# A spectral and FFN kernel on one core: another order of the first loads, a buffer per scaled matrix, and one block of dummy products

## Chip, cores, metric

The kernel runs on one core of one Trainium2 chip. The metric is device time in microseconds (us), less is better. Engines are named as in the profile: PE (TensorE products), PEld (its weight loads), DVE (VectorE), ACT (ScalarE), POOL (GpSimd), SP (SyncE, which here only issues DMAs).

## What is computed

x is 2048 x 448 in bf16 (batch 1). Two kinds of layer alternate, each with a residual sum around it:

```python
def _A_ref(x, w_r, w_i):
    X = rfft2(x.astype(float32)); X = X * (w_r + 1j * w_i)
    return irfft2(X, s=(S, D)).astype(bfloat16)
def _B_ref(x, w1, b1, w2, b2):
    h = einsum("bsd,df->bsf", x, w1) + b1
    r = where(h > 0, h, 0)
    return einsum("bsf,fd->bsd", r * r, w2) + b2
x = x + _A_ref(layernorm(x), A_w_r, A_w_i)
x = x + _B_ref(layernorm(x), B_w1, B_b1, B_w2, B_b2)
# and both once more with the same weights
```

w_r and w_i are 2048 x 225, w1 is 448 x 1792, w2 1792 x 448. The layernorm has no parameters (eps 1e-5).

## The kernel before

x lies in SBUF as 16 tiles of 128 rows x 448 (partition p holds the rows 16p to 16p+15, tile t is the t-th of each). The Fourier transforms are products with constant matrices, in stages:

- **A1** (`ln_stats` L774, `minus` L803, `first_A` L816): for each tile or pair of tiles (GROUPS1) the mean and the variance, on DVE (bn_stats, bn_aggr) or, for tiles 1, 4 and 6, on ACT (two passes with an accumulator, L781); a square root on ACT, a reciprocal on DVE; then FA (a 16-point transform, 128 x 256) is scaled by the reciprocal (`scaled`, L668, written to a buffer Fs of which there are four, t % NFS). A product on PE is five matmuls of 256 columns: four with the tile, one that subtracts the mean. The result is evacuated to XA by ACT or DVE.
- **TD** multiplies XA along the columns (TD_sb), first the half with tiles 0 to 7, then the one with 8 to 15; it needs the tiles of its half. **B** is the second transform along the rows (G_sb). **W** is the multiplication by w_r and w_i on DVE (`stage_W`, L946). It reads Wt: slots loaded by DMA (Wp), and slots that POOL copies (tags M) out of two gathers (`gather`, L700, tag pool.yT) which fetch the mirrored rows of w_i and w_r.
- **Bi**, **TI**, **AI** go back, with H_sb, HS_sb, TI_sb and FI_sb. **ln**, **h** and **o** are the FFN. Then A2 to AI and the FFN once more.

The order of the work is written out by hand. Every piece of work is a unit with a tag, such as `A1.0`; the table ORDER gives for each tag the ranks of its units, in the order in which the code makes them. A letter behind a rank chooses the engine (a ACT, d DVE, p POOL). Each engine runs its units in the order of rank, in order; a unit waits by semaphores for what it reads and for buffers. For a single tile on DVE the units of `A1.t` are: statistics, aggregate, square root (ACT), reciprocal, minus (-2 x mean), scaled matrix, product (PE), evacuation. For a pair such as `A1.14`: statistics and aggregate of the first tile, of the second, root, reciprocal, minus, then scaled matrix, product and evacuation of the first and of the second.

`schedule` (L415) walks the ranked units with estimated durations. It chooses the PSUM bank (8 of them) for each product, and where PE would by its estimate stand idle it puts in dummies (`warm_mm`, L1306): matmuls of a matrix of ones into a free bank, whose result nobody reads.

The loads (`dma`, L616) go out on SP's and ACT's queues. Before:

```python
for n, (a, b, e) in enumerate(((0, 1, "sp"), (1, 2, "act"), (2, 3, "sp"), (4, 8, "act"), (3, 4, "sp"), (8, 12, "act"),
                               (12, 16, "sp"))):
    dma(e, xin[:, a:b, :], x_dram[:, a:b, :])
    if n == 2: dma("sp", FA_sb[:], dc["FA"])
```

so SP issues x0, x2, FA, x3 and x12 to 15, ACT x1, x4 to 7, a first use of its square root (which loads its table), and x8 to 11. All weight loads (G, TD, Wt, H, HS, ...) are on SP behind these and wait for x4 (`x4`, L747); so do the gathers on POOL.

Of the kernel before, what the change touches and what calls it, by code (L numbers as in the profile page):

```python
# [10 lines left out]
P = 128  # L11
# [30 lines left out]
def make_constants():  # L42
# [71 lines left out]
    for g, M in enumerate((cl * np.cos(th), cl * np.sin(th))):  # L114
# [1270 lines left out]
```

## Time and profile before

| | |
|---|---|
| runs | 266.96 us median of 3 (266.46, 266.96, 268.15) |
| profiled execution | span 267.8 us from the first to the last instruction; its own time is not listed beside it |
| busy | PE 259.3 (97%), PEld 158.9 (59%), DVE 212.7 (79%), ACT 171.3 (64%), POOL 14.4 (5%) |
| dummies | 16, of 512 columns, the last begins at 11.5 us |
| DMA | 17.03 MB, mean 64 GB/s |
| the most waited for | ACT arena on PE 17.7 us, DVE arena on ACT 17.6 us, both spread over the whole span |

Busy time of PE includes the dummies and is modelled where matmuls overlap, so 97% doesn't say that PE is the bound everywhere. In the lines of a timeline the columns are: start, busy time, engine, line, operation, output<-input, shape, count, and in brackets the idle time before with what ended it. The lines of DMA issues have the size of each and the time from issue to landing. A "q" behind an engine is its sequencer, which issues DMAs.

### The profile page before, as it was taken

The page shows a single profiled execution, that of the slowest core. Times are in us where ns is not written, and L with a number is a line of the kernel's source. Part 1 is how long each engine was busy: PE and PEld are TensorE (multiplying, and loading weights), DVE is VectorE, ACT ScalarE, POOL GpSimd, SP SyncE. Part 2 cuts the span into 40 slices and gives each one's busy share as a digit, 9 for nine tenths or more (in the row PEclk, how much of TensorE's full clock was granted, in tenths as well). Part 3 has the DMA queues.
Part 4 walks back from the last instruction along what each step waited for, and adds up shares of the span by engine and source line. Part 5 has one row for each costly group of instructions (what it writes and reads, how often), then busy time and mean ns, then how long its engine had stood idle before and what let it go on. Part 6 is the DMA issues. An engine that isn't in the chain of part 4 may idle for free. (4 is left out here: it accounts for less than half of the span.)

```text
span 267.8 us, 5840 instructions
## 1 busy us (share of the span) xinstructions
PE 259.3 (97%) x2194; PEld 158.9 (59%) x2194; DVE 212.7 (79%) x652; ACT 171.3 (64%) x391; POOL 14.4 (5%) x42
## 2 busy tenths in 40 slices
PE   6899999899999999999999999989999999999996
PEld 1477665798544544555559774779654554454554
DVE  5866999899996964999999899899998963463722
ACT  4688994979429755985128896889735753678000
POOL 0577000000000000000000000000000000000000
PEclk9999999999999999999999999999999999999999
DMA  6999370020420222300000000011232026200211
GB/s 222 305 376 354 74 228 17 0 42 10 54 52 2 39 43 44 68 0 0 2 0 4 2 2 0 2 23 22 39 73 42 0 42 111 89 2 0 70 39 47
DMA packets 27312, 17.03 MB, mean 64 GB/s; under 512 B 20210, under 2 KB 25810, under 8 KB 27156
## 3 DMA queue, kind: packets, MB, share of 16 engines
q1 hardware_dynamic: 26692, 14.82, 21.7%
q10 hardware_dynamic: 432, 1.03, 1.1%
q0 software_dynamic: 160, 0.81, 0.8%
q8 instruction: 17, 0.28, 0.5%
q14 instruction: 11, 0.09, 0.1%
HBM read 11.15 MB, written 1.84 MB: 48 GB/s over the span
## 5 line engine op out<-in xcount | busy, mean ns | idle before, releaser
L636 PE MATMUL ps<-yT,W_sb 64*128 64x512 bf16 (+1 forms) x770 | 90.3, 346 | 0.0
L636 PE MATMUL ps<-W_sb,arena 128*128 128x448 bf16 (+2 forms) x490 | 87.5, 336 | 0.0
L636 PEld LDWEIGHTS ps<-yT,W_sb 64*128 64x128 bf16 (+1 forms) x770 | 51.5, 95 | 36.0 <-issue 1.5
L636 PEld LDWEIGHTS ps<-W_sb,arena 128*128 128x128 bf16 x490 | 46.3, 98 | 36.3 <-DVE arena L688 0.8
L655 ACT ACTIVATE arena<-ps,b1col 128x512 bf16<-128x512 f32 x84 | 51.9, 691 | 14.2 <-PE ps L636 14.0
L688 DVE TENSOR_TENSOR arena<-arena 128x512 bf16<-128x512 bf16 (+1 forms) x140 | 45.7, 367 | 18.0 <-ACT arena L655 17.6
L1109 ACT ACTIVATE VT<-x_sb 128x448 bf16<-128x448 bf16 x32 | 18.4, 577 | 13.4 <-DVE x_sb L1085 13.3
L661 ACT ACTIVATE arena<-ps 128x448 bf16<-128x448 f32 (+1 forms) x44 | 25.1, 693 | 2.4 <-PE ps L636 2.2
L1205 DVE SCALAR_TENSOR_TENSOR x_sb<-ps,arena 128x448 bf16<-128x448 f32 (+2 forms) x27 | 15.2, 570 | 14.1 <-PE ps L636 13.7
L655 ACT ACTIVATE mv<-mv,epst 128x1 f32<-128x1 f32 (+1 forms) x46 | 12.6, 294 | 17.2 <-DVE mv L794 12.1
L655 ACT ACTIVATE arena<-ps 128x256 bf16<-128x256 f32 x56 | 17.8, 392 | 4.0 <-PE ps L636 3.7
L661 ACT ACTIVATE XA<-ps 128x512 bf16<-128x512 f32 x29 | 15.6, 592 | 3.2 <-PE ps L636 3.2
L661 ACT ACTIVATE VT<-ps 128x512 bf16<-128x512 f32 (+1 forms) x26 | 13.0, 567 | 7.0 <-PE ps L636 6.9
L636 PE MATMUL ps<-yT,VT 64*128 64x512 bf16 x42 | 15.8, 376 | 0.0
L636 PE MATMUL ps<-HS_sb,arena 128*128 128x512 bf16 x64 | 14.9, 380 | 0.1
L636 PE MATMUL ps<-arena,G_sb 128*128 128x448 bf16 (+1 forms) x76 | 14.4, 333 | 0.5 <-ACT arena L661 0.4
L672 ACT ACTIVATE arena<-x_sb,rstd 128x448 bf16<-128x448 bf16 x11 | 7.2, 666 | 10.5 <-DVE rstd L1124 6.0
L636 PE MATMUL ps<-TD_sb,XA 112*64 112x112 bf16 (+2 forms) x312 | 13.2, 224 | 0.0
L636 PE MATMUL ps<-Fs,xin 128*128 128x256 bf16 x64 | 10.0, 290 | 3.0 <-DVE mv L784 2.9
L636 PEld LDWEIGHTS ps<-TD_sb,XA 112*64 112x64 bf16 (+2 forms) x312 | 12.1, 108 | 1.1 <-issue 0.6
L688 DVE TENSOR_TENSOR tmp<-arena,Wt 128x896 bf16<-128x896 bf16 (+1 forms) x14 | 11.4, 852 | 1.7 <-ACT arena L661 1.5
L1135 DVE SCALAR_TENSOR_TENSOR arena<-x_sb,mv,b2row 128x448 bf16<-128x448 bf16 x16 | 10.7, 679 | 0.1
(76 smaller groups left out, 300.9 us busy)
## 6 DMA issues: line engine op xcount, KB each, us to landing
out_dram<-x_sb SPq DMA_DIRECT2D x15, 112.0 KB, 1.7
W_sb<-in_B_w_dram SPq DMA_DIRECT2D x1, 1568.0 KB, 16.1
W_sb<-in_B_w_dram SPq DMA_DIRECT2D x1, 1344.0 KB, 6.7
HS_sb<-c_HS SPq DMA_DIRECT2D x1, 1024.0 KB, 11.2
G_sb<-c_G SPq DMA_DIRECT2D x1, 960.0 KB
xin<-in_A_x_dram ACTq DMA_DIRECT2D x2, 448.0 KB, 5.4
xin<-in_A_x_dram SPq DMA_DIRECT2D x1, 448.0 KB
Wt<-in_A_w_i_dram SPq DMA_DIRECT2D x1, 392.0 KB, 4.7
```

Source lines behind the costliest of these rows:

```text
L636: return sch.add("pe", lambda e: e.matmul(_res(o), lhsT, rhs, start=start, stop=stop, skip_group_check=skip), [lhsT, rhs], [o], cost=cost, ...
L655: sch.add("act", lambda e: e.activation(o, _res(i), func, **kw), rd, [o], cost=c)
L661: op = sch.add(engs[0], lambda e: e.activation(o, _res(i), ACT.Copy) if h[0].eng == "act" else e.tensor_copy(o, _res(i)), [i], [o], cost=c ...
L672: op = sch.add(engs[0], lambda e: e.activation(o, i, ACT.Copy, scale=s) if h[0].eng == "act" else e.tensor_scalar(o, i, s, 1.0, op0=ALU.mu ...
L688: sch.add(eng, lambda e: e.tensor_tensor(o, _res(a), b, op), [a, b], [o], cost=_free(o) / rate + 69.0)
L1109: sch.add("act", lambda e, i=i, o=o, x=x: e.activation(o, x, ACT.Square, accum_out=mv[:, i, 4:5]), [x], [o, mv[:, i, 4:5]], cost=560.0)
L1135: small(lambda e, o=o, x=x, m=m: e.scalar_tensor_tensor(out=o, in0=x, scalar=m, in1=b2row[:], op0=ALU.add, op1=ALU.add), [x, m, b2row[:]], ...
L1205: small(lambda e: e.scalar_tensor_tensor(out=o, in0=_res(i), scalar=r[0] if r else 1.0, in1=xb[:, t, d0:d1], op0=ALU.mult, op1=ALU.add), [ ...
```

## The change

1. x is loaded in 12 pieces instead of 7: tiles 0 to 7 one by one, then pairs. SP has x0, x2, x3, x5, x6, x7, then 8-9, 10-11, 12-13, 14-15; ACT has x1, FA and x4, and after these the first use of its square root.
2. The weight loads of SP wait for x7 instead of x4. The gathers still wait for x4.
3. The scaled FA of tile t is written to `x_sb[:, t, 0:2 * P]`, not to one of four Fs. (x_sb of a tile is written next in stage AI. Stage A2 keeps Fs.)
4. `schedule` has no estimates any more: banks stand in ORDER behind a colon, and dummies in WARM: 13 of 512 columns and one of 128, into bank 7, right before the unit of rank 35, which is the product of tile 0. There are no other dummies.
5. ORDER is a new table. From rank 511 on it is the old one with 5 added to each rank (there are five more loads). Before that, the units of the first layer and of the start of the FFN are in another order, and some are on another engine.

```diff
 ORDER = {
-    "dve.warm": "1", "dve.epst": "4", "sp.xin": "0 12 15 18", "act.xin": "11 14 17", "sp.FA_sb": "13",
-    "act.warm": "16", "pool.ones": "8", "pool.back": "10", "dve.x_sb": "3", "dve.W1_sb": "5", "pool.yT": "92 52",
...
-    "M.6": "249 248", "dve.arena": "2", "sp.J_sb": "281", "sp.TD_sb": "65", "sp.G_sb": "76 19",
-    "sp.Wt": "143 38 182 37", "sp.H_sb": "217 216", "sp.HS_sb": "181", "sp.TI_sb": "240", "sp.FI_sb": "279",
-    "sp.b2row": "282", "sp.b1in": "280", "dve.b1col": "420", "sp.W1_sb": "232 230 231 233", "sp.W2_sb": "223",
-    "A1.0": "6 7 24 26 9p 28d 64 99a", "A1.1": "23 25 30 32 39 27d 70p 71 111a", "A1.2": "20 21 29 34 22p 67p 68 78a",
...
-    "A1.12": "117 119 115 118 124 128 132p 129d 133 144a 130d 136 137d",
-    "A1.14": "101 104 84 103 107 116 113p 126p 127 131d 122p 125 138a", "TD0.0": "142 148d 146 147a",
-    "B0.0": "156 157a 158 159a", "W0.0": "163 166 168 167 170 169", "TD0.1": "140 151a 149 153a",
...
+    "dve.warm": "0", "dve.epst": "4", "sp.xin": "5 8 9 12 23 24 25 26 47 90", "act.xin": "6 10", "act.FA_sb": "7",
+    "act.warm": "11", "pool.ones": "2", "pool.back": "15", "dve.x_sb": "14", "dve.W1_sb": "1", "pool.yT": "67 33",
...
+    "M.6": "207 173", "dve.arena": "3", "sp.J_sb": "205", "sp.TD_sb": "63", "sp.G_sb": "60 39",
+    "sp.Wt": "84 78 140 120", "sp.H_sb": "104 182", "sp.HS_sb": "123", "sp.TI_sb": "142", "sp.FI_sb": "106",
+    "sp.b2row": "122", "sp.b1in": "50", "dve.b1col": "342", "sp.W1_sb": "170 156 246 294", "sp.W2_sb": "242",
+    "A1.0": "16 17 20 22 18p 34p 35:0 72a", "A1.1": "13 27 31 38 46 21p 57p 66:3 107a",
+    "A1.2": "19 28 29 36 41d 37p 42:1 109a", "A1.3": "30 43 44 49 52p 55d 61:2 88a",
+    "A1.4": "32 40 51 56 64 76p 70p 82:0 91a", "A1.5": "45 58 71 74 87p 79p 101:5 141a",
+    "A1.6": "53 81 102 111 116 96p 126p 132:6 146a", "A1.7": "48 54 59 68 69d 77p 93:4 143a",
+    "A1.8": "62 73 65 75 85 86 94p 97d 108:2 155a 95p 112:0 121a",
+    "A1.10": "83 92 80 89 98 100 103p 110p 115:3 127a 113p 131:1 144d",
+    "A1.12": "105 117 99 114 118 124 134d 129p 135:7 152a 136p 147:0 149a",
+    "A1.14": "125 130 119 128 137 138 133d 145p 150:1 154d 139d 148:3 151d", "TD0.0": "159:3 166d 161:7 162a",
+    "B0.0": "167:4 181d 169:3 175a", "W0.0": "199 200 201 202 204 203", "TD0.1": "157:0 160d 164:5 165a",
...
+WARM = {35: ((7, 512), (7, 512), (7, 512), (7, 512), (7, 512), (7, 512), (7, 512), (7, 512), (7, 512), (7, 512), (7,
+    512), (7, 512), (7, 512), (7, 128))}
...
     def schedule(self):
...
+        for n, u in enumerate(self.ranked()):
+            for b, w in WARM.get(n, ()):
+                d = _Op("pe", self.warm_fn(b, w), False, 0.0, 0.0)
+                take(b, d)
...
-        for n, (a, b, e) in enumerate(((0, 1, "sp"), (1, 2, "act"), (2, 3, "sp"), (4, 8, "act"), (3, 4, "sp"), (8, 12, "act"),
-                                       (12, 16, "sp"))):
+        for n, (a, b, e) in enumerate(((0, 1, "sp"), (1, 2, "act"), (2, 3, "sp"), (3, 4, "sp"), (4, 5, "act"), (5, 6, "sp"),
+                                       (6, 7, "sp"), (7, 8, "sp"), (8, 10, "sp"), (10, 12, "sp"), (12, 14, "sp"),
+                                       (14, 16, "sp"))):
             dma(e, xin[:, a:b, :], x_dram[:, a:b, :])
-            if n == 2:
-                dma("sp", FA_sb[:], dc["FA"])
-            if n == 3:
+            if n == 1:
+                dma("act", FA_sb[:], dc["FA"])
+            if n == 4:
                 sch.add("act", lambda e: e.activation(warm[:, 0:1], warm[:, 0:1], ACT.Sqrt), [warm[:, 0:1]], [warm[:, 0:1]],
...
-        x4 = [xin[:, 4, :]]
+        x4 = [xin[:, 7, :]]
...
-                x, f = xin[:, t, :], Fs[:, t % NFS, :]
+                x, f = xin[:, t, :], x_sb[:, t, 0:2 * P]
                 scaled(f, FA_sb[:], r, EV["FS"])
```

In the tags of SP, G has two loads (its columns from 6 on, 960 KB, then the first six, 192 KB) and Wt four (w_r and w_i for the rows of 1 to 7, 392 KB each, then the two of 112 KB for rows 0 and 8), with their ranks in that order.

More of the change, by code (lines that the diff above doesn't have):

```diff
@@ L327 @@
     DMA_RATE = 350.0
-    TURN = (200.0, 100.0)
-    SLACK = 60.0
-    DMA_SLACK = 200.0
-    BEGIN = 800.0
-    WINDOW = 3413.0
     def __init__(self):
@@ L342, in __init__ @@
         self.lead = {}
-        self.warm_from = 0.0
-        self.cold_until = 0.0
-        self.warm_share = 0.7
     def add(self, eng, fn, reads=(), writes=(), is_dma=False, cost=100.0, lat=130.0, unit=None):
@@ L403, in ranked @@
             if u.tag in ORDER:
-                w = ORDER[u.tag].split()[k]
+                w = ORDER[u.tag].split()[k].split(":")
+                for t, b in zip(u.tiles, w[1] if len(w) > 1 else ""):
+                    t.bank = int(b)
+                w = w[0]
                 if w[-1].isalpha():
@@ L415, in schedule, with take @@
     def schedule(self):
-        free = dict.fromkeys(self.ENGINES, self.BEGIN)
-        free["pe"] = self.warm_from
-        bank_free = [0.0] * NB
-        bank_user = [None] * NB
-        dma_free = 0.0
-        rows = 128
-        used = []
-        done = {}
-        def ready(op):
-            r = 0.0
-            for d in op.gdeps:
-                if d.unit is op.unit or (d.eng == "pe" and op.eng == "pe"):
-                    continue
-                if d.is_dma:
-                    r = max(r, done[d] + 130.0 + self.DMA_SLACK)
-                else:
-                    r = max(r, done[d] + d.lat + (80.0 if op.eng == "pe" else 0.0) + (self.SLACK if d.eng != op.eng else 0.0))
-            return r
-        def pick(n, now, taken):
-            best = None
-            for b in range(0, NB, n):
-                if any(i in taken for i in range(b, b + n)):
-                    continue
-                if all(bank_user[i] is None or all(op in done for op in bank_user[i].readers) for i in range(b, b + n)):
-                    f = max(bank_free[b:b + n])
-                    key = (max(f, now), n == 1 and bank_free[b ^ 1] <= now, f)
-                    if best is None or key < best[0]:
-                        best = (key, b)
-            assert best is not None, "no bank is free"
-            return best[1]
-        for u in self.ranked():
-            e = u.eng
-            first = free[e] + (self.TURN[u.rows < 128] if e == "pe" and u.rows != rows else 0.0)
-            taken = []
-            for w in u.tiles:
-                now = max(first, ready(u.ops[0])) + sum(op.cost for op in u.ops[:u.ops.index(w.first)])
-                w.bank = pick(w.n, now, taken)
-                taken += range(w.bank, w.bank + w.n)
+        user = [None] * NB
+        def take(b, op):
+            if user[b] is not None:
+                op.deps.extend(r for r in user[b].readers if r not in op.deps)
+        for n, u in enumerate(self.ranked()):
+            for b, w in WARM.get(n, ()):
+                d = _Op("pe", self.warm_fn(b, w), False, 0.0, 0.0)
+                take(b, d)
+                if not self.ops["pe"]:
+                    d.deps.extend(self.warm_deps)
+                self.ops["pe"].append(d)
             for op in u.ops:
-                t = max(first if op is u.ops[0] else free[e], ready(op))
                 for w in u.tiles:
@@ L461, in schedule @@
                         for i in range(w.bank, w.bank + w.n):
-                            old = bank_user[i]
-                            if old is not None:
-                                t = max(t, bank_free[i] + 80.0 + self.SLACK)
-                                for rd in old.readers:
-                                    if rd not in op.deps:
-                                        op.deps.append(rd)
-                            bank_user[i] = w
-                if e == "pe" and op is u.ops[0]:
-                    while t - free["pe"] >= 120.0:
-                        f = free["pe"]
-                        cold = f < self.cold_until
-                        recent = sum(min(b, t) - max(a, t - self.WINDOW) for a, b in used[-90:] if b > t - self.WINDOW)
-                        if not (cold or recent < self.warm_share * self.WINDOW):
-                            break
-                        n = next((n for n in (512, 256, 128) if (n / 2.4 + 2.5) * (2.0 if cold else 1.0) + 60.0 <= t - f), 0)
-                        if not n:
-                            break
-                        b = min(((bank_free[b], b) for b in range(NB) if b not in taken and (
-                            bank_user[b] is None or all(x in done for x in bank_user[b].readers))), default=None)
-                        if b is None:
-                            break
-                        if b[0] > f:
-                            free["pe"] = b[0]
-                            continue
-                        c = (n / 2.4 + 2.5) * (2.0 if cold else 1.0)
-                        d = _Op("pe", self.warm_fn(b[1], n), False, c, 195.0)
-                        if bank_user[b[1]] is not None:
-                            d.deps.extend(bank_user[b[1]].readers)
-                        if not self.ops["pe"]:
-                            d.deps.extend(self.warm_deps)
-                        self.ops["pe"].append(d)
-                        used.append((f, f + c))
-                        free["pe"] = f + c
-                    t = max(t, free["pe"])
-                    begin = t
@@ L497, in schedule @@
-                t += op.cost
-                free[e] = t
-                done[op] = t
-                self.ops[e].append(op)
-                if op.is_dma:
-                    done[op] = dma_free = max(dma_free, t + 1800.0) + op.lat
-                    if e == "pool":
-                        done[op] = max(dma_free, t + 7000.0)
-                for w in op.takes:
-                    for i in range(w.bank, w.bank + w.n):
-                        bank_free[i] = max(bank_free[i], t + op.lat)
@@ L508, in schedule @@
-            if e == "pe":
-                rows = u.rows
-                used.append((begin, free["pe"]))
-        self.length = max(done.values())
-        self.used = used
-        self.done = done
+                            take(i, op)
+                            user[i] = w
+                self.ops[u.eng].append(op)
         for e in self.ENGINES:
@@ L722, in bass_interleave_layers__spectral_gfnet__dense_activation_squared_relu__prompt_kernel @@
         memset(epst[:, 0:1], EPS)
-        for n, (a, b, e) in enumerate(((0, 1, "sp"), (1, 2, "act"), (2, 3, "sp"), (4, 8, "act"), (3, 4, "sp"), (8, 12, "act"),
-                                       (12, 16, "sp"))):
+        for n, (a, b, e) in enumerate(((0, 1, "sp"), (1, 2, "act"), (2, 3, "sp"), (3, 4, "sp"), (4, 5, "act"), (5, 6, "sp"),
+                                       (6, 7, "sp"), (7, 8, "sp"), (8, 10, "sp"), (10, 12, "sp"), (12, 14, "sp"),
+                                       (14, 16, "sp"))):
             dma(e, xin[:, a:b, :], x_dram[:, a:b, :])
-            if n == 2:
-                dma("sp", FA_sb[:], dc["FA"])
-            if n == 3:
+            if n == 1:
+                dma("act", FA_sb[:], dc["FA"])
+            if n == 4:
                 sch.add("act", lambda e: e.activation(warm[:, 0:1], warm[:, 0:1], ACT.Sqrt), [warm[:, 0:1]], [warm[:, 0:1]],
-                        cost=200.0)
+                        cost=1480.0)
         memset(ones[:], 1.0, eng="pool")
         sch.warm_deps = sch.lead["pool"] = [sch.last_write[k] for k in _pages(ones[:])][:1]
-        sch.warm_from = 1000.0
-        sch.cold_until = 4800.0
         sch.add("pool", lambda e: e.iota(back[:, 0:1], pattern=[[0, 1]], base=(16 * (P - 1) + 9) * 225, channel_multiplier=-16 * 225), [],
```

172 rows, old and new, of the table ORDER are left out of this document.

## The prediction

> **What bounds the kernel now.** I read the span by windows of 5 us first, because a mean over 268 us hides the one stage that the change touches, and then the timeline of PE and DVE inside that stage.
>
> ```profile
> 0.00:5.00 5.00, 4.02 (x9) 1.19 (x9) 2.65 (x7) 2.96 (x7) 0.67 (x7) 1.00 0.61 177
> 5.00:10.00 5.00, 2.05 (x9) 1.19 (x9) 3.39 (x15) 2.44 (x10) 2.53 (x5) 1.00 0.97 319
> 10.00:15.00 5.00, 5.00 (x30) 3.13 (x28) 3.83 (x20) 2.50 (x11) 2.13 (x6) 1.00 1.03 338
> 15.00:20.00 5.00, 4.95 (x44) 3.85 (x41) 3.50 (x15) 4.73 (x12) 4.13 (x12) 1.00 1.06 367
> 20.00:25.00 5.00, 5.00 (x44) 4.11 (x44) 2.68 (x5) 4.01 (x9) 2.91 (x10) 1.00 1.05 359
> 25.00:30.00 5.00, 5.00 (x42) 3.84 (x41) 4.65 (x9) 4.84 (x11) 2.06 (x5) 1.00 0.69 185
> 30.00:35.00 5.00, 4.54 (x40) 2.77 (x39) 4.96 (x9) 5.00 (x9) 0.00 (x0) 1.00 0.51 146
> 35.00:40.00 5.00, 4.93 (x37) 3.21 (x36) 5.00 (x8) 4.86 (x10) 0.00 (x0) 1.00 0.76 196
> 40.00:45.00 5.00, 4.93 (x26) 2.19 (x25) 4.83 (x9) 1.13 (x2) 0.00 (x0) 1.00 0.09 23
> ```
>
> Columns: window, length, busy time of PE, PEld, DVE, ACT and POOL, PE clock, DMA share, GB/s. Two things stand out. The DMA engines are full (share 0.97 to 1.06) from 5 to 25 us. And DVE is full from 25 to 45 us: that is the multiplication by the weights (stage W), and its start therefore sets the end of the spectral layer. When does it start, and why?
>
> ```profile
> 0.72 0.87 SPq L628 DMA_DIRECT2D xin<-in_A_x_dram  x2
> 0.98 4.02 PE L1307 MATMUL ps<-ones 128*128 128x512 bf16 x9 [0.98 <-POOL ones L709]
> 3.31 0.63 DVE L793 BATCH_NORM_STATS2 st<-xin 128x6 f32<-128x448 bf16 x1 [0.28 <-DMA xin<-in_A_x_dram]
> 7.52 0.28 DVE L673 TENSOR_SCALAR Fs<-FA_sb,rstd 128x256 bf16<-128x256 bf16 x1 [0.73 <-DMA FA_sb<-c_FA]
> 7.62 1.23 POOL L704 DMA_INDIRECT yT<-in_A_w_i_dram,back  x1 [0.65 <-POOL m L805]
> 7.95 1.01 PE L636 MATMUL ps<-Fs,xin 128*128 128x256 bf16 x4 [2.95 <-DVE mv L784]
> 8.97 3.19 PE L1307 MATMUL ps<-ones 128*128 128x512 bf16 x7
> 11.96 1.06 PE L636 MATMUL ps<-Fs,xin 128*128 128x256 bf16 x4
> 13.02 0.60 PE L636 MATMUL ps<-Fs,xin 128*128 128x256 bf16 x4
> 13.57 0.60 PE L636 MATMUL ps<-Fs,xin 128*128 128x256 bf16 x4
> 21.15 2.46 PE L636 MATMUL ps<-TD_sb,XA 128*128 128x224 bf16 x24
> 25.21 1.61 DVE L688 TENSOR_TENSOR tmp<-arena,Wt 128x896 bf16<-128x896 bf16 x2 [1.55 <-ACT arena L661]
> ```
>
> Dummies run to 5.00, PE idles 2.95 us, one product runs at 7.95, seven dummies fill 8.97 to 11.96, and only then do fifteen products follow one another, 1.06 us for the slow first, then one every 0.55 us (13.02 to 13.57). TD begins at 21.15, call that T, and stage W 4.06 us later at 25.21. So the late first product and the second block of dummies are what delay T now. From 25.21 on I take the rest as rigid: stage W's nearly 20 us of DVE work do not change, nor does the work behind them; only ranks and banks do. A shift of T is then a shift of the end. The listed ending chain starts only at 163.79 us, so it neither supports nor contradicts this.
>
> **The change, part by part.** *Start.* FA goes from third on SP's queue to second on ACT's, and no 448 KB load stands beside it. An unhindered 112 KB load is read 2.6 us after its issue (0.72 to 3.31), issues are 0.45 us apart, so x1, FA and x4 land near 3.5, 3.8 and 4.3. ACT's table then loads one issue, 0.45 us, later; whatever of that x1's statistics feel lies in the shade of the wait found below. The first scaled matrix moves to POOL, where the order puts the first gather, a wait for x4, ahead of it: about 4.7 + 1.23 (gather) + 0.48 (the scaling, row below), that is 6.4 us. Thirteen and a quarter dummies at 4.02 / 9 = 0.447 us end at 0.98 + 5.9 = 6.9 if PE stays slow, so the first product comes at 6.4 to 6.9 instead of 7.95, and no dummies follow it.
>
> *Buffers.* A scaled matrix in each tile's own row of x_sb takes away the waits of Fs for an older product. x_sb is written again only after TI; this costs nothing.
>
> *Products up to the last load.* DVE's order has eleven statistics ahead of those of tile 15, and some 26 small operations and two scaled matrices.
>
> ```profile
> L793 DVE BATCH_NORM_STATS2 st<-xin x13: 587/607/628, 3.3 to 17.8; 128x6 f32<-128x448 bf16 x13
> L673 POOL TENSOR_SCALAR Fs<-FA_sb,rstd x10: 471/482/489, 9.1 to 18.4; 128x256 bf16<-128x256 bf16 x10
> 9.04 0.24 DVE L794 BATCH_NORM_AGGREGATE mv<-st 128x2 f32<-128x6 f32 x2
> ```
>
> 3.31 + 11 x 0.607 + 26 x 0.12 + 2 x 0.28 = 13.7; with half a microsecond of waits for ACT's square roots, 14.2. Twelve products (0 to 11) are out by about 15.4. So far the change gains four microseconds or more.
>
> *The last x load.* Here it is lost, by my reading. In the new order SP issues x0, x2, x3, x5, x6, x7, x8-9, x10-11, the small G, x12-13, **b1in**, the large G, TD, two loads of Wt and only **then** x14-15. Before, all of x stood ahead of all weights. Nothing waits on SP but the small G (for x7, about 5.7), so x14-15 is issued near 10 us; what counts is what stands ahead of it. Do loads of one queue pass each other?
>
> ```profile
> 9.30 1.40 SPq L628 DMA_DIRECT2D HS_sb<-c_HS  x1
> HS_sb<-c_HS SPq DMA_DIRECT2D x1, 1024.0 KB, 11.2
> Wt<-in_A_w_r_dram SPq DMA_DIRECT2D x1, 112.0 KB, 11.2
> G_sb<-c_G SPq DMA_DIRECT2D x1, 960.0 KB
> G_sb<-c_G SPq DMA_DIRECT2D x1, 192.0 KB
> TD_sb<-c_TD SPq DMA_DIRECT2D x1, 224.0 KB, 6.4
> Wt<-in_A_w_i_dram SPq DMA_DIRECT2D x1, 392.0 KB, 4.7
> Wt<-in_A_w_r_dram SPq DMA_DIRECT2D x1, 392.0 KB
> xin<-in_A_x_dram SPq DMA_DIRECT2D x3, 112.0 KB, 4.6
> FA_sb<-c_FA SPq DMA_DIRECT2D x1, 64.0 KB, 5.9
> q0 software_dynamic: 160, 0.81, 0.8%
> ```
>
> (The last row is POOL's queue: packets, MB, share.) A load of 112 KB behind HS took 11.2 us to land: they do not. So I count bytes. Up to and with x14-15: x 1792, FA 64, G 1152, TD 224, Wt 784, together 4016 KB (of 1024) = 4.11 MB, and both gathers, 0.81 MB, which POOL issues by about 8: 4.92 MB. The windows above move 0.885, 1.595 and 1.690 MB, 4.17 MB by 15.0, then 0.367 per us: 4.92 at 17.05. How far behind the count does a landing lie? HS: ahead of it and with it x, FA, G, the 392 and 112 KB of w_i, TD, the 392 of w_r, itself and one gather, 5.68 MB, reached at 19.1; it landed at 9.30 + 11.2 = 20.5, 1.4 us behind. And b1in, which nobody needs before the FFN:
>
> ```profile
> 37.50:38.00 0.50, 0.43 (x4) 0.15 (x3) 0.50 (x2) 0.50 (x3) 0.00 (x0) 1.00 1.25 49
> 38.00:38.50 0.50, 0.50 (x3) 0.08 (x3) 0.50 (x2) 0.50 (x3) 0.00 (x0) 1.00 0.72 35
> 34.05 3.95 SPq L628 DMA_DIRECT2D J_sb<-c_J  x1
> b1in<-in_B_b_dram SPq DMA_DIRECT2D x1, 3.5 KB, 7.2
> ```
>
> It is 3.5 KB in 1792 single elements; while it passes, the engines are full and move 35 to 49 GB/s, for about 1 us. I take 1.05 (bounds 0.3, and 2.0 if the blocked issue behind it, as J's, leaves a hole). The landing L of x14-15 is then 17.05 + 1.4 + 1.05 = **19.5**. Bounds: 16.7 (second gather behind it, 0.403 / 0.367 = 1.1 less, b1in 0.3, lag 0.4), and 20.5 (b1in at 2.0). Splitting x into smaller loads is inside these.
>
> *What is late next.* DVE meets the statistics of tile 15 at 14.2 and waits about 5 us, and behind them in DVE's order stand the reciprocal of tiles 12 and 13, the statistics of 14, and everything on to W; ACT's square root for 14 and 15 holds three evacuations of finished tiles behind it too. After L: 2 x 0.607, three or four small operations, then product 12 at L + 1.85, 13, 15 (its bank waits for an evacuation by DVE, L + 3.0) and 14, each 0.55 us: T = L + 4.1 = 23.6. TD to W has the same links as before, 4.1: W at 27.7 against 25.21, **2.5 us later**. POOL's copies of the gathered columns, eight ahead of the one W needs, begin at about L + 2.6 and fit.
>
> *Ranks after TI.* From rank 511 on they are the old ones plus five; between TI and there, h and ln units are reordered. I see no wait added or removed: 0, bounds -0.7 and +0.7.
>
> **Sum.** Gain of the start up to product 11: spent in waiting for x14-15. Profiled execution: 267.8 + 2.5 = 270.3. It stands 0.84 above the median of the runs, 266.96; with that kept, **269.5 us**.
>
> **The rivals.**
>
> *PE slow again after the wait.* PE would idle from 15.4 to L + 1.85 = 21.35, 6 us, and could come back at the slow rate of the beginning.
>
> ```profile
> L636 PEld LDWEIGHTS ps<-Fs,xin x64: 95/98/151, 7.9 to 20.8; 128*128 128x128 bf16 x64
> ```
>
> A weight load takes 151 ns in the slow state and 95 to 98 later, though the clock column says 1.00 throughout. The trace has PE slow at the beginning and fast from the product at 13.02 on; it shows no idle time of 6 us after that, so it doesn't tell. From the block that began at 8.97, work was slow for 4.05 us; half of that, 2.0 us, is lost on a stretch where PE sets T: 271.5, up to 272.8. [...] I give it less than the plain case, since L may be early enough to make the gap short.
>
> *x14-15 not late: faster.* If the pair reaches the core by 14.2, because the engines serve it between the weights or the weights' issues are held up and x gets past, T = 14.2 + 4.1 = 18.3, W at 22.4, 2.8 us earlier: 264.2. For it: three x loads of SP landed in 4.6 us beside larger loads of ACT's queue. Against it: the 11.2 us of 112 KB in the same queue. It decides wherever L is below 17.0.
>
> *No change.* L near its lower bound, 16.7 to 17.3: gain and wait cancel, 267.0.
>
> *The dummies don't do what they say.* If PE turns fast inside them they end early, near 5.5, and a gap stands ahead of the first product. With DVE waiting for x14-15 that costs nothing; without the wait, a few slow products, 0.5 us each at most. It has no chance of its own and changes no forecast.
>
> **How the numbers follow.** Chances: late load, PE fast, 0.50 (own range 268.0 to 270.8); late load, PE slow again, 0.22; load not late, 0.14; no change, 0.14. One per cent, 2.7 us, is about what a measurement of this kernel tells from no change; the border is 269.6, so the first case is split, 0.24 over and 0.26 within. Slower 0.24 + 0.22 = 0.46; same 0.26 + 0.14 = 0.40; faster 0.14. The range 264.1 to 272.6 leaves out half of the third case and a third of the second.
>
> **What would show it.** Right: statistics of tile 15 on DVE begin near 19.5 after a wait of about 5 us for xin; PE idles between some product and product 12; TD begins near 23.6, W near 27.7, and TI shifts by as much. First product at 6.4 to 6.9 with no dummies behind it. Slow again: weight loads of 151 ns after the gap. Wrong: no wait for xin on DVE after 10 us, or TD before 20.

## The result, and the profile after

The changed kernel takes **274.99 us** (median of 4 runs, 274.39 to 275.72), the kernel before 266.98 in the runs beside it: a ratio of **1.0281** (95% interval 1.0244 to 1.0318), slower by 8.0 us. The prediction was 269.5, slower, with a range up to 272.6: the direction is right, the size isn't. The profiled execution took 274.39 us, and its span is 272.6; in every later run too the time is 1.7 to 1.9 us more than the span.

First the windows of 5 us of the kernel after. The columns are those of the prediction: PE, PEld, DVE, ACT, POOL, PE clock, DMA share, GB/s.

```profile
0.00:5.00 5.00, 4.02 (x10) 1.49 (x11) 3.38 (x10) 2.82 (x8) 0.86 (x8) 1.00 0.58 141
5.00:10.00 5.00, 2.44 (x13) 1.32 (x11) 4.26 (x16) 3.38 (x14) 3.00 (x6) 0.86 0.88 279
10.00:15.00 5.00, 5.00 (x39) 4.08 (x38) 3.43 (x17) 3.64 (x10) 4.11 (x12) 0.80 1.05 295
15.00:20.00 5.00, 1.97 (x19) 1.52 (x16) 0.24 (x2) 1.39 (x4) 0.69 (x2) 1.00 1.10 342
20.00:25.00 5.00, 2.89 (x15) 2.10 (x16) 2.82 (x10) 2.41 (x6) 3.17 (x9) 0.72 1.04 311
```

From 15 to 20 us all five columns of engines collapse while the DMA engines are full: everybody waits for a load. And the clock column falls twice, at 5 to 15 and at 20 to 25 us; before, it stood at 1.00 in every window. The timelines of PE, then DVE (in all timelines of PE below, the short line of each product's fifth matmul, `ps<-x_sb,m`, is left out; a count such as x12 at the end of one is that of the part shown):

```profile
0.98 5.09 PE L1228 MATMUL ps<-ones 128*128 128x512 bf16 x14 [0.98 <-POOL ones L631]
8.63 1.01 PE L558 MATMUL ps<-x_sb,xin 128*128 128x256 bf16 x4 [2.56 <-POOL x_sb L595]
9.65 1.06 PE L558 MATMUL ps<-x_sb,xin 128*128 128x256 bf16 x4
...
16.26 0.60 PE L558 MATMUL ps<-x_sb,xin 128*128 128x256 bf16 x4
22.11 0.92 PE L558 MATMUL ps<-x_sb,xin 128*128 128x256 bf16 x4 [5.14 <-POOL x_sb L595]
23.03 1.06 PE L558 MATMUL ps<-x_sb,xin 128*128 128x256 bf16 x4
...
25.96 2.46 PE L558 MATMUL ps<-TD_sb,XA 128*128 128x224 bf16 x24
```

```profile
15.24 0.16 DVE L715 BATCH_NORM_AGGREGATE mv<-st 128x2 f32<-128x6 f32 x1
20.70 0.63 DVE L714 BATCH_NORM_STATS2 st<-xin 128x6 f32<-128x448 bf16 x1 [5.30 <-DMA xin<-in_A_x_dram]
...
29.88 1.30 DVE L610 TENSOR_TENSOR tmp<-arena,Wt 128x896 bf16<-128x896 bf16 x2
```

DVE stands 5.30 us for x14-15, until 20.70; call that L. PE idles 5.14 us, then takes 1.06 us for a product that took 0.55 before the gap: it has come back slow. T is 25.96 and W 29.88. The queue of SP shows the load behind everything that the new order puts ahead of it, and the timelines of ACT and POOL show what delays the start:

```profile
0.72 3.72 SPq L550 DMA_DIRECT2D xin<-in_A_x_dram  x8
6.68 0.33 SPq L550 DMA_DIRECT2D G_sb<-c_G  x1
7.05 0.43 SPq L550 DMA_DIRECT2D xin<-in_A_x_dram  x1
...
12.26 2.59 SPq L550 DMA_DIRECT2D xin<-in_A_x_dram  x1
```

```profile
5.90 0.58 ACT L702 ACTIVATE yT<-xin 128x448 bf16<-128x448 bf16 x1 [0.64 <-DMA xin<-in_A_x_dram]
...
6.78 1.16 POOL L626 DMA_INDIRECT yT<-in_A_w_i_dram,back  x1 [2.15 <-DVE mv L715]
8.00 0.94 POOL L595 TENSOR_SCALAR x_sb<-FA_sb,rstd 128x256 bf16<-128x256 bf16 x2
```

x4 is read at 5.90, the gather runs from 6.78, the first scaled matrix from 8.00, the first product from 8.63. The gather's row names DVE as what it waited for, but in e11, where DVE's aggregate is long done, it starts at 7.76 behind 3.08 us of waiting for a load of x: x4 is the wait.

### The profile page after: what moved, and what is told of

It reads as the page before. It is cut to its first block, busy times and chain, and to the rows that moved or that the text cites. A ratio compares the mean times of both kernels' runs of the same rounds, so it can differ in the third digit from the quotient of the medians.

```text
span 272.6 us, 5811 instructions
## 1 busy us (share of the span) xinstructions
PE 260.1 (95%) x2192; PEld 163.5 (60%) x2192; DVE 214.0 (79%) x652; ACT 170.8 (63%) x390; POOL 14.6 (5%) x43
## 5 line engine op out<-in xcount | busy, mean ns | idle before, releaser
L558 PEld LDWEIGHTS ps<-yT,W_sb 64*128 64x128 bf16 (+1 forms) x770 | 54.6, 95 | 32.6 <-issue 1.5
L577 ACT ACTIVATE arena<-ps,b1col 128x512 bf16<-128x512 f32 x84 | 51.8, 691 | 14.3 <-PE ps L558 14.1
L610 DVE TENSOR_TENSOR arena<-arena 128x512 bf16<-128x512 bf16 (+1 forms) x140 | 44.9, 364 | 17.4 <-ACT arena L577 17.1
L583 ACT ACTIVATE arena<-ps 128x448 bf16<-128x448 f32 (+1 forms) x41 | 24.2, 697 | 4.6 <-PE ps L558 4.4
L1126 DVE SCALAR_TENSOR_TENSOR x_sb<-ps,arena 128x448 bf16<-128x448 f32 (+2 forms) x27 | 15.2, 569 | 14.2 <-PE ps L558 13.9
L577 ACT ACTIVATE mv<-mv,epst 128x1 f32<-128x1 f32 (+1 forms) x46 | 12.8, 295 | 20.3 <-DVE mv L715 17.7
L558 PE MATMUL ps<-x_sb,xin 128*128 128x256 bf16 x64 | 12.1, 332 | 7.7 <-POOL x_sb L595 7.7
L558 PEld LDWEIGHTS ps<-x_sb,xin 128*128 128x128 bf16 x64 | 7.5, 119 | 10.3 <-issue 8.3
L714 DVE BATCH_NORM_STATS2 st<-xin 128x6 f32<-128x448 bf16 x13 | 7.8, 608 | 6.4 <-DMA xin<-in_A_x_dram 6.4
```

The lines of the kernel that those rows point to most:

```text
L558: return sch.add("pe", lambda e: e.matmul(_res(o), lhsT, rhs, start=start, stop=stop, skip_group_check=skip), [lhsT, rhs], [o], cost=cost, ...
L577: sch.add("act", lambda e: e.activation(o, _res(i), func, **kw), rd, [o], cost=c)
L583: op = sch.add(engs[0], lambda e: e.activation(o, _res(i), ACT.Copy) if h[0].eng == "act" else e.tensor_copy(o, _res(i)), [i], [o], cost=c ...
L610: sch.add(eng, lambda e: e.tensor_tensor(o, _res(a), b, op), [a, b], [o], cost=_free(o) / rate + 69.0)
L714: small(lambda e, si=si, xi=xi: e.bn_stats(si, xi), [xi], [si], (c1 - c0) / 0.96 + 69.0)
L1126: small(lambda e: e.scalar_tensor_tensor(out=o, in0=_res(i), scalar=r[0] if r else 1.0, in1=xb[:, t, d0:d1], op0=ALU.mult, op1=ALU.add), [ ...
```

## The experiments

Two theories stood at the beginning. **A**: the place of x14-15 in SP's queue costs nearly everything, by the bytes ahead of it, and PE at half its clock after the wait adds something. **B**: the other parts of the change (the small loads of x, b1in, the gather ahead of the scaling, the buffers) cost a good share. Ratios are to runs of the kernel before made beside each row, on the same chip.

| run | edit, against | L | T | span | span - T | time, us | ratio |
|---|---|---|---|---|---|---|---|
| before, of the prediction | | - | 21.15 | 267.8 | 246.7 | | |
| b_again | none, before | - | 18.29 | 265.3 | 247.0 | 267.06 | |
| after | the change, before | 20.70 | 25.96 | 272.6 | 246.6 | 274.99 | 1.0281 (1.0244-1.0318) |
| after_again | none, after | 20.98 | 26.61 | 273.5 | 246.9 | 275.31 | 1.0260 (1.0226-1.0295) |
| e1_x_first | x14-15 early, after | 15.18 | 18.85 | 265.5 | 246.7 | 267.79 | 0.9984 (0.9960-1.0008) |
| e4_half | x14-15 ahead of two Wt, after | 18.01 | 21.63 | 268.2 | 246.6 | 270.07 | 1.0082 (1.0054-1.0110) |
| e2_b1_late | b1in late, after | 20.58 | 26.21 | 272.9 | 246.7 | 274.38 | 1.0220 (1.0154-1.0286) |
| e3_fill | dummies in the wait, after | 20.97 | 24.59 | 271.2 | 246.6 | 273.55 | 1.0219 (1.0147-1.0291) |
| e9_gather2 | second gather late, after | 20.47 | 26.10 | 273.4 | 247.3 | 273.20 | 1.0176 (1.0144-1.0208) |
| e11_big_pieces | fewer loads of x, after | 21.71 | 27.34 | 274.0 | 246.7 | 274.95 | 1.0251 (1.0221-1.0281) |
| e12_guard4 | weights wait for x4, after | 19.62 | 25.25 | 272.2 | 247.0 | 273.91 | 1.0216 (1.0166-1.0266) |
| e6_fill_first | 8 dummies more, e1 | 14.71 | 19.18 | 265.8 | 246.6 | 267.07 | 0.9947 (0.9930-0.9964) |
| e5_gather_late | first gather late, e1 | 13.88 | 18.29 | 264.9 | 246.6 | 267.14 | 0.9962 (0.9948-0.9976) |
| e8_best | TD early, b1in late, e5 | 13.87 | 17.72 | 264.6 | 246.9 | 266.69 | 0.9957 (0.9934-0.9980) |

L (start of the statistics of tile 15 on DVE), T (first TD on PE) and the span are those of the profiled execution, the time is the median (b_again is a single run). Rows that were not run side by side are compared with care: the kernel before had medians from 266.98 to 268.25 us beside them. Side by side ran e1, e2 and e3; e4, e5 and e6; after_again, e9, e11 and e8. **span - T is 246.6 to 247.3 us in all fourteen**: nothing behind T answers to any of these edits, and a row of this table is explained when its T is.

**b_again**, the kernel before once more.

> The kernel before once more, for a second profile. Theory (the first profile was of an untypically slow execution, about 3 us over its own typical one, since the changed kernel's span lies 1.8 us below its time while the 267.8 of before lies above the times): span near 265, PE fast one stretch earlier (by about 9.5 instead of 13 us), T near 18 to 19 instead of 21.15. Rival (the profile was typical, and what lies around the span differs by kernel): span 267.5 to 268, T near 21.1.

Measured: span 265.3, PE's timeline:

```profile
0.98 3.79 PE L1307 MATMUL ps<-ones 128*128 128x512 bf16 x9 [0.98 <-POOL ones L709]
6.58 0.60 PE L636 MATMUL ps<-Fs,xin 128*128 128x256 bf16 x4 [1.81 <-DVE mv L784]
7.12 1.67 PE L1307 MATMUL ps<-ones 128*128 128x512 bf16 x7
8.94 0.60 PE L636 MATMUL ps<-Fs,xin 128*128 128x256 bf16 x4
...
18.29 1.89 PE L636 MATMUL ps<-TD_sb,XA 128*128 128x224 bf16 x18
```

The seven dummies that took 3.19 us in the execution which I had predicted from take 1.67 here: PE turned fast already in the first nine. T is 18.29 instead of 21.15. With 1.8 us beside the span, the first execution corresponds to a time of 269.6, in the upper tail of the kernel before (266.98 to 269.65 in the 13 runs beside it; the one of 269.65 has a span of 267.8).

**e1_x_first**: undo the position alone.

```diff
-    "sp.xin": "5 8 9 12 23 24 25 26 47 90"
+    "sp.xin": "5 8 9 12 23 24 25 26 47 47"
```

> The changed kernel with x14-15 issued right behind x12-13, ahead of b1in, the large G, TD and Wt; nothing else. Theory (the late load and the slow PE after it cost the time): no wait of DVE for xin after 10 us, the product of tile 12 follows that of tile 6 at about 17, T near 19.4 instead of 25.96, stage W near 23.3 instead of 29.88, time 274.99 - 6.5 = 268.4. Rival (W then waits for Wt or for POOL's copies of the gathers, which were hidden): T early but W not before 27, time 272 or more.

Measured 267.79 us, no wait for x on DVE. PE:

```profile
8.46 0.60 PE L558 MATMUL ps<-x_sb,xin 128*128 128x256 bf16 x4 [2.03 <-POOL x_sb L595]
...
9.75 1.06 PE L558 MATMUL ps<-x_sb,xin 128*128 128x256 bf16 x4
...
18.85 1.31 PE L558 MATMUL ps<-TD_sb,XA 128*128 128x224 bf16 x12
```

One rank takes 7.1 us off T (25.96 to 18.85) and 7.2 off the time (by the ratios 3.0%, some 8 us). W follows at 22.77, 3.9 us behind T as in after: neither Wt nor the copies hold it. The rest of the change together is neutral to within half a per cent: theory A. But the gain at the start that I had expected is not there either: the first product comes at 8.46, and PE turns slow within the second one.

**e4_half**: x14-15 ahead of only the two Wt loads (`90` becomes `77`).

> The kernel after, with the load of x14 and x15 ahead of only the last two weight loads (0.80 MB less in front of it), still behind b1in, the large G and TD. If the load is late by the bytes that are queued in front of it, it lands 0.80 MB / 0.342 MB per us = 2.3 us sooner: the statistics of tile 15 start at 18.0 to 18.6 us instead of 20.70, TensorE's gap before the product of tile 12 shrinks from 5.1 to some 2.8 us, the first TD starts at 22.0 to 23.6, and the time is about 271.8 us. If it is something else that holds it (b1in, the time that SP's queue needs to issue), the statistics stay past 20 us and the time is 274 or more.

DVE, then PE:

```profile
18.01 0.63 DVE L714 BATCH_NORM_STATS2 st<-xin 128x6 f32<-128x448 bf16 x1 [3.44 <-DMA xin<-in_A_x_dram]
```

```profile
8.88 0.60 PE L558 MATMUL ps<-x_sb,xin 128*128 128x256 bf16 x4 [3.38 <-POOL x_sb L595]
...
19.42 0.60 PE L558 MATMUL ps<-x_sb,xin 128*128 128x256 bf16 x4 [3.19 <-POOL x_sb L595]
...
21.63 2.46 PE L558 MATMUL ps<-TD_sb,XA 128*128 128x224 bf16 x24
```

0.80 MB less ahead, L 2.69 us sooner (2.3 worked out). The time, 270.07, is below what was expected, and T is 4.33 us sooner, more than L: PE stays fast behind both its gaps here, and T - L is 3.62 instead of 5.26.

**e2_b1_late**: b1in behind TI's load (`sp.b1in` from 50 to 143).

> The changed kernel with b1in issued behind TI's load instead of ahead of the large G; x14-15 stays behind Wt. Theory (b1in's single elements hold SP's queue up for 1.0 to 2.5 us): x14-15 lands at 18.2 to 19.7 instead of 20.7, time 272.5 to 274.0, or 271.5 if the shorter idle time of PE leaves it fast. Rival (b1in passes beside other work): less than 0.3 us.

L is 20.58: b1in is not what makes the load late. Without it more bytes pass first, and fewer behind. SP's queue, then the windows:

```profile
9.65 6.25 SPq L550 DMA_DIRECT2D xin<-in_A_x_dram  x1
```

```profile
10.00:15.00 5.00, 5.00 (x36) 3.89 (x35) 3.39 (x17) 3.20 (x9) 4.07 (x12) 0.73 0.97 378
15.00:20.00 5.00, 1.97 (x19) 1.51 (x16) 0.24 (x2) 1.39 (x4) 0.68 (x2) 0.95 0.98 282
```

378 GB/s instead of 295 from 10 to 15 us, but 282 instead of 342 behind it: the issue of x14-15 alone held SP for 6.25 us, until 15.90, where it ended at 14.85 in after. What holds it there I can't say. In the time, e2 is 0.6 us below after and 0.9 below after_again, by the ratios 0.4 to 0.6%; all of that is inside the intervals, so a cost of b1in in the time is neither shown nor excluded.

**e3_fill**: 24 dummies right before the product of tile 12.

```diff
-    512), (7, 512), (7, 512), (7, 128))}
+    512), (7, 512), (7, 512), (7, 128)), 135: ((7, 512),) * 24}
```

> The changed kernel with 24 dummies of 512 columns ahead of the product of tile 12, in the time in which PE waits for x14-15; the load stays late. Theory (PE turned slow again in the wait): the last four products take 0.55 us each, T = landing + 4 instead of landing + 5.3, time about 273.5. Rival (PE's speed is hidden behind the evacuations by ACT and DVE): below 0.4 us, or slower if the dummies run over the landing.

```profile
17.00 5.34 PE L1228 MATMUL ps<-ones 128*128 128x512 bf16 x24
22.38 0.60 PE L558 MATMUL ps<-x_sb,xin 128*128 128x256 bf16 x4
...
24.59 1.60 PE L558 MATMUL ps<-TD_sb,XA 128*128 128x224 bf16 x15
```

The same load as late as before (20.97), but four products at 0.55 us each: T - L is 3.62 instead of 5.26 (5.63 in after_again). PE at half its clock behind the wait thus costs 1.6 to 2.0 us of T. The time is 1.4 us below after's, which is inside the intervals; T - L carries the reading.

**after_again**, the kernel after once more, beside e9, e11 and e8.

> The kernel after, unchanged, so that the variants of this call are compared with it on the same chip. Its statistics of tile 15 start between 20 and 21 us, TensorE is slow (1.06 us a product) in the first three or four products and again in the last four, and the time is 274 to 276 us. Every kernel so far had its span 246.4 to 247.0 us above the start of the first TD; so does this one.

275.31; four slow products behind the wait again (22.39 to 26.61). One expectation fell: the first products ran at 0.55 us from 8.77 on, behind a gap of 1.96 us. So the slow spell at the start comes and goes with the execution; the one behind the long wait doesn't.

**e9_gather2**: GpSimd's second gather 6.6 us later than in after (9.71 to 16.36; `pool.yT` from "67 33" to "114 33").

> The kernel after, with GpSimd's second gather (0.40 MB) issued some 4 us later, so that its data come behind the load of x14 and x15 instead of ahead of it. If every byte that is moved ahead of that load counts, whichever queue it is in, the load lands 0.40 / 0.342 = 1.2 us sooner: the statistics of tile 15 start at 19.4 to 19.7 us, the first TD 1.2 us sooner, and the time is 1.2 us below the kernel after on this chip. The rival: only the bytes of SP's own queue count. Then the statistics stay at 20.5 to 20.9 us and the time is that of after.

The time is 2.1 us below after_again's. In the profiled execution L is only 20.47, but that execution (275.2) is the slowest of its four, and its weight loads start late. SP and DVE:

```profile
7.64 0.33 SPq L550 DMA_DIRECT2D G_sb<-c_G  x1
...
20.47 0.63 DVE L714 BATCH_NORM_STATS2 st<-xin 128x6 f32<-128x448 bf16 x1 [4.07 <-DMA xin<-in_A_x_dram]
```

From the issue of the small G, L is 12.8 us away, against 14.0 in after (6.68 to 20.70) and 14.1 in after_again (6.83 to 20.98): the 1.2 us of the 0.40 MB. Counted so, bytes of another queue count; L itself is only 0.2 to 0.5 us sooner, not at the 19.4 to 19.7 expected. In the time, 2.1 us, the effect is larger than in the trace; where the rest comes from I can't say.

**e11_big_pieces**: x5 to x7 in one load, x8 to x11 in one load.

> The kernel after, with tiles 5 to 7 in one load and tiles 8 to 11 in one load instead of five (rows of 2688 and 3584 bytes instead of 896 and 1792). The load of x14 and x15 came 1.2 us later than I had worked out from the byte curve of before; if that is because the small x loads move fewer bytes in the first 7.5 us (232 and 294 GB/s after, 312 and 372 before), some 0.2 to 0.4 MB more are moved by then, the statistics of tile 15 start at 19.6 to 20.1 us, and the time is 0.6 to 1.2 us below after's. The rival: the hole of 163 to 172 GB/s at 10 to 12 us decides, or the queue's issue. Then the statistics stay at 20.5 to 20.9.

```profile
7.95 0.33 SPq L550 DMA_DIRECT2D G_sb<-c_G  x1
...
21.71 0.63 DVE L714 BATCH_NORM_STATS2 st<-xin 128x6 f32<-128x448 bf16 x1 [5.41 <-DMA xin<-in_A_x_dram]
```

It falls: the time doesn't change (274.95 against 275.31), and in the profiled execution L is later, as x7, for which the weights wait, comes later inside its larger load (small G issued at 7.95, in after_again at 6.83). The size of the pieces isn't what was missing. The two rows put another suspect in its place: L moves with the moment at which the weights are released.

**e12_guard4**: the weight loads wait for x4, as before the change.

```diff
-        x4 = [xin[:, 7, :]]
+        x4 = [xin[:, 4, :]]
```

> The kernel after, with SP's weight loads waiting for x4 as before instead of x7. In after, SP issues nothing from 4.44 to 6.68 us, for it waits for tile 7. If that hole is part of the lateness of x14 and x15, the small G is issued 0.6 to 1.0 us sooner (5.7 to 6.1 us), the statistics of tile 15 start as much sooner, at 19.7 to 20.2 us, and the time is 0.6 to 1.0 us below after's 1.026 of before, at a ratio near 1.023. If the DMA engines are the limit, busy with the x loads anyway, the statistics stay at 20.5 to 21.0 and the ratio at 1.026; x5 to x7 could even land later.

```profile
5.78 0.33 SPq L550 DMA_DIRECT2D G_sb<-c_G  x1
...
19.62 0.63 DVE L714 BATCH_NORM_STATS2 st<-xin 128x6 f32<-128x448 bf16 x1 [4.30 <-DMA xin<-in_A_x_dram]
```

Release 0.90 us sooner, L 1.08 sooner, the time 1.1 below that of after and 1.4 below after_again's, not run side by side. That is no more than the intervals; the two rows carry it. From the issue of the small G to L it is 13.8 to 14.2 us in all six runs that change neither the gathers nor the place of x14-15 (after 14.0, after_again 14.1, e2 13.9, e3 14.2, e11 13.8, e12 13.8), although that issue itself moves from 5.78 to 7.95.

**e6_fill_first** and **e5_gather_late** look for the gain at the start, both on e1. e6 adds eight dummies ahead of the first product; e5 moves the first gather behind the second scaled matrix (`pool.yT` to "67 38"). In e5, e8 and e11 the key of WARM moves too (35 to 34 or 32), because it counts units and fewer of them now stand ahead of the first product.

> The kernel with x14 and x15 behind x12 and x13, and eight more dummies of 512 columns ahead of the first product. The first product stays near 8.5 us, for the gather is still ahead of it. If TensorE is slow in the first products because it idled 2.0 us before them, they now take 0.55 us each instead of 1.06, the first TD starts near 17.9 us and the time is about 267.0. The rival: the slow products are not what sets the first TD (VectorE and ScalarE do), or TensorE is slow there for another reason: first TD 18.5 to 19.0, time 267.8.

> The kernel with x14 and x15 behind x12 and x13, and on GpSimd the first gather moved behind the second scaled matrix. If the gather ahead of the scaling is what sets the first product at 8.46 us, that product starts at 6.1 to 6.5 us, with no idle time of TensorE over 1 us between the dummies and it, the first products take 0.55 us each instead of 1.06, the first TD starts at 17.3 to 18.3 us instead of 18.85 and the time is 266.3 to 267.3 us. The rival: VectorE's statistics and ScalarE's roots set the first TD anyway, it stays at 18.5 to 19.0 and the time at 267.8.

PE in e6, then in e5:

```profile
9.11 0.60 PE L558 MATMUL ps<-x_sb,xin 128*128 128x256 bf16 x4 [0.74 <-POOL x_sb L595]
...
19.18 2.46 PE L558 MATMUL ps<-TD_sb,XA 128*128 128x224 bf16 x24 [0.53 <-DMA TD_sb<-c_TD]
```

```profile
6.41 0.60 PE L558 MATMUL ps<-x_sb,xin 128*128 128x256 bf16 x4
...
18.29 2.46 PE L558 MATMUL ps<-TD_sb,XA 128*128 128x224 bf16 x24 [0.39 <-DMA TD_sb<-c_TD]
```

Both stay fast: the mean granted clock is 1.00 in all five timed runs of each (0.999 once), where it was 0.987 to 0.994 in nine of ten runs of e1. (T of e6's profiled execution, 19.18, misses the 17.9 expected: that execution, 267.58, is the slowest of its five, the first gather, which waits for x4, starts in it at 7.25 instead of e1's 6.61, and T waits 0.53 us for TD's load.) In e5 the first product comes where the prediction had it, right behind the dummies, and T waits for a new partner, TD's load.

**e8_best** takes that wait away: e5, TD's load ahead of the large G, b1in late.

> The kernel with x14 and x15 behind x12 and x13, GpSimd's first gather behind the second scaled matrix, TD's load ahead of the large G and b1in behind the load of TI. In the run without the last two edits the first TD waited 0.39 us for TD's load and was at 18.29; with TD 1 MB earlier in the queue it starts right behind the last product, at 17.6 to 18.0 us, and the time is 266.2 to 266.9 us, below both kernels. The rival: the product of G, or the first product of the weights, then waits for the large G or for Wt in TD's place, and the time stays at 267.1.

```profile
7.11 0.60 PE L558 MATMUL ps<-x_sb,xin 128*128 128x256 bf16 x4 [0.59 <-POOL x_sb L595]
...
17.72 2.46 PE L558 MATMUL ps<-TD_sb,XA 128*128 128x224 bf16 x24
```

T 17.72, 266.69 us (266.13 to 268.11): below both kernels, 0.9957 of before, and by the medians 3.1% below after_again beside it. The intervals of e5, e6 and e8 overlap, so which of the three is best is not settled.

## Why the prediction was wrong

**Right: the mechanism and its place.** x14-15 behind the weights, DVE's wait of about 5 us (5.30), PE's gap before the product of tile 12, the gain up to product 11 spent in the wait, the shift of the end as a whole. The count of bytes as a measure of lateness is right too (e4: 2.3 us worked out, 2.7 measured), across queues as well if L is counted from the release of the weights (e9), and so is the cost of nothing for the new ranks after TI: span - T doesn't change. The buffers were not tried by themselves (with four of them the new order would wait for itself: tile 10's scaled matrix, rank 110 on POOL, for the product of tile 6 from the same buffer, rank 132, whose own scaled matrix stands behind on POOL, rank 126); their cost is bounded only as a part of e1's neutral rest.

**Failed: "It stands 0.84 above the median ..., with that kept".** I read the span of 267.8 as a time. It belongs to a time of about 269.6, an execution in which PE was slow until 13 us. So I measured the loss of T from an untypical 21.15 and added it to the median of ordinary executions. From my own T of 23.6 the sum is 23.6 + 246.65 (267.8 - 21.15) + 1.8 = 272.0: **2.5 us** of the error, ahead of any physics. The clue was in the quoted rows: seven dummies in 3.19 us, with 1.00 in the clock column.

**Failed: the rival "PE slow again", at 0.22.** It came in six of the seven profiled executions with a late load and nothing to fill the gap; the seventh is e4, with a gap of 3.19 us (e9's gap of 3.12 us was followed by slow products all the same). T - L is 5.26, where I had 4.1; fast, it would have been 3.6. That is **1.2 us** of the error (25.96 - 20.70 - 4.1). I had put it below the plain case since L might be early enough to make the gap short. That a shorter gap leaves PE fast was my estimate, and it held only in some executions: 3.12 us (e9) and 2.56 us (after) were followed by slow products as 5.14 was, 3.38 and 3.19 us (e4) were not.

**Mis-sized: L, 19.5 instead of 20.70, 1.2 us.** The byte curve of before was laid over the new order as it was, though in it the weights are released by x4 (small G at 6.02) and after the change by x7; the prediction put that at "about 5.7", it came at 6.68. That is 1.0 of the 1.2 us, for L stands 14 us behind this release (e12, e11). With the old guard L is 19.62 (e12). That 19.5 came so near is partly luck: 1.05 of it was b1in, and with b1in out of the way L was the same.

The sum: 269.5 + 2.5 + 1.2 + 1.2 = 274.4, the time of the profiled execution; the median lies 0.6 higher, which no term here explains.

**Failed, at no cost here: the first product at "6.4 to 6.9".** x4 was put at 4.3 and read at 5.90; the gather, which needs it, held the first scaled matrix on POOL until 8.00. Behind the wait for x14-15 that is hidden. Without the wait it is a reason why e1 gains nothing: e5, which moves the gather, is 0.65 us below e1, though the intervals overlap. Likewise "the dummies end early, a gap stands ahead of the first product": it did (6.07 to 8.63), and cost nothing with the wait, about 0.7 us without it (e1 267.79, e6 267.07, not run side by side; the intervals of the ratios overlap a little).

**The other rivals**: "x14-15 not late" and "no change" needed L at 14.2 and 17.3 or less; it was 20.70.

## What to carry to other kernels

Move a load in a full queue only after counting the bytes ahead of it in all queues and the moment that releases them; 0.8 MB were 2.7 us here, and the gap that a late load leaves is paid a second time when TensorE comes back slow, with 1.6 to 2.0 us of T here. Before a profiled execution serves as the baseline, hold its own time, or the duration of one repeated instruction in it, against the median's. A faster start shows only when the next wait in line is gone as well: here first x14-15, then the gather ahead of the scaling, then TD's load.

## What the runs showed of the hardware

- **PE's spells at half its clock.** Behind gaps of 4.1 to 6.3 us there was a slow spell of three to five products (1.06 us each at its slowest, instead of 0.55) every time (after 5.14, after_again 6.27, e2 5.02, e9 4.29, e11 4.16 and 5.13, e12 4.14). Behind gaps of 1.8 to 3.4 us it came in some executions (after 2.56, e1 2.03, e12 2.00, e2 2.19, e3 2.46, e9 3.12) and not in others (b_again 1.81, after_again 1.96, e4 3.38 and 3.19). So the length of the gap alone doesn't decide in the range from 1.8 to 3.4 us; what else does, no run shows. The slow products often begin one or two products late (e11: two at 0.55 us, then three of 1.01 to 1.07).
- **The clock column does not show PE's slow stretch at the start**: 1.00 while dummies of 512 columns took 447 ns each (before; in e3 24 of them took 5.34 us in a fast stretch, 223 ns each). The later spells it does show, at 0.50 (after, from 9 to 12 and from 23 to 25 us).
- **One load's issue can hold SP for over 6 us.** That of x14-15 took 6.25 us in e2, where the six loads ahead of it were issued within 3.0 us (6.64 to 9.62), and 2.59 in after, where the seven ahead of it took 5.5 (6.68 to 12.21). No run shows what it waits for.
